# Two loads of the fourth row block of x are put behind a one-column memset on GpSimd

## The chip, the cores and the metric

The kernel runs on one core of a Trainium2 chip. The metric is the device time of one execution in microseconds (us). TensorE (PE, with its weight loads as PEld), VectorE (DVE), ScalarE (ACT), GpSimd (POOL) and SyncE (SP) run side by side. Transfers are issued from the queues of SP, ACT and POOL.

## What is computed

Two branches over the same input x (2048 rows of 512) are mixed by a gate, all in float32:

```python
def _A_ref(x, wqkv, w_phi, wo):          # linear attention, 32 heads of 16
    qkv = (lambda x, *d: x.transpose(*d))((x @ wqkv).reshape(B, S, 3, H, Dh), 2, 0, 3, 1, 4)
    q, k, v = qkv[0], qkv[1], qkv[2]
    pq = jnp.einsum("bhsd,hdf->bhsf", q, w_phi)
    pk = jnp.einsum("bhsd,hdf->bhsf", k, w_phi)
    phi_q = jnp.concatenate([_softmax(pq, axis=-1), _softmax(-pq, axis=-1)], axis=-1)
    phi_k = jnp.concatenate([_softmax(pk, axis=-1), _softmax(-pk, axis=-1)], axis=-1)
    kv = jnp.einsum("bhsf,bhsd->bhfd", phi_k, v)
    z  = jnp.einsum("bhsf->bhf", phi_k)
    num = jnp.einsum("bhqf,bhfd->bhqd", phi_q, kv)
    den = jnp.einsum("bhqf,bhf->bhq", phi_q, z)[..., None] + 1e-6
    o = num / den
    return (lambda x, *d: x.transpose(*d))(o, 0, 2, 1, 3).reshape(B, S, D) @ wo

def _B_ref(x, w1, b1, w2, b2):           # 512 -> 1792 -> 512, squared relu
    h = jnp.einsum("bsd,df->bsf", x, w1) + b1
    r = jnp.where(h > zero, h, zero)
    return jnp.einsum("bsf,fd->bsd", r * r, w2) + b2

g = _sigmoid((x * gate_w).sum(-1, keepdims=True))
return g * a + (1 - g) * b
```

## The kernel before

**Precision.** Each float32 operand is split into a high and a low part (`split`, lines 63 and 66: ACT copies the high part, DVE subtracts it from the source), and a product takes three matmuls (high by high, high by low, low by high). Such a triple stands at lines 76 to 78, or at 653 to 655 in the function `block`.

**Work in rounds.** x is cut into four blocks of 512 rows, b = 0 to 3, each as four tiles of 128x512 (k = 0 to 3). `work_list` walks twice over the four blocks, with seven of the fourteen chunks of the hidden layer each time. Each entry does an up product (`u`) and adds its down products into four sums (`d`). In the first walk the products for k and v run in between, for eight pairs of 128-row chunks (p = 0 to 7). The function `at(slot, f)` hangs each step on a half slot, and a scheduler makes one fixed order of instructions for each engine from it. An engine goes through its own list in order.

**A pair.** A pair p takes seven blocks of 128x512 products, i = 1, 2, 6, 5, 7, 3, 4, in banks pX and pY. Blocks 6, 7, 3 and 5 read sums and differences of x tiles instead of x. For these, `sums_load` (line 608) brings the pair's 128 rows of each x tile in two transfers of 256 KB, in runs of 512 bytes, and `sums_add` makes them with four additions, lines 615 to 618, on GpSimd for every pair but the first. `sums` then splits the result on ACT (`sh`) and DVE (`sl`).

**Weights that come back.** The weights of blocks 1, 6 and 3 don't stay on the chip. They lie in DRAM (`wkeep`, six tiles of 512 KB) and go round through three slots, named sloto twice (slots o0 and o1 here) and slotez. Once a tile has been used, `again` (line 641) issues from the ACT queue the load of the tile that is due three steps later into its slot. So within a pair block 1 reads o0 and o1, block 6 reads ez and then o0, block 3 reads o1 and then ez.

**The staging ring.** All transfers into tiles tagged `in` go through a ring of four buffers of 256 KB. A load waits until the splits or additions that read the buffer before are done. Around the change the ring is used in this order: the four tiles of x block 2 (loaded from the GpSimd queue, line 576), the two row tiles of pair 2, the four tiles of x block 3, and the two row tiles of pair 3. The loads of x block 3 are issued from the SP queue by the function `load`, line 86, called at line 582. Their first two tiles (k = 0, 1) take the buffers of the last two tiles of x block 2, and the other two (k = 2, 3) those of pair 2's rows. x block 3 is split at `x_split`, and first read by the products of pair 4.

Of the kernel before, what the change touches and what calls it, by code (L numbers as in the profile page):

```python
# [7 lines left out]
F32 = mybir.dt.float32  # L8
# [7 lines left out]
P = 128  # L16
S, D, H, DH, F = 2048, 512, 32, 16, 1792
NK = D // P
SB = 512
NB = S // SB  # L20
# [14 lines left out]
def tile_gated_mix(ctx: ExitStack, tc: tile.TileContext, xT, xn, wqT, wkT, wphi, wv, wo, w1, b1, w2, b2, gw, out):  # L35
    nc = tc.nc
    pool = lambda name, bufs, **kw: ctx.enter_context(tc.tile_pool(name=name, bufs=bufs, **kw))
    const = pool("const", 1)
    stage = pool("stage", 4)
# [44 lines left out]
    def load(src, eng=nc.sync):  # L84
        t = stage.tile([P, 512], F32, tag="in", name="in")
        st["in"] = eng.dma_start(t, src)
        return t
# [32 lines left out]
    st, up_w, down_w = {}, {}, {}  # L120
# [136 lines left out]
    def gate_load(n):  # L257
        eng, pin = ((nc.sync, "in" if n > 1 else "wv"), (nc.gpsimd, "summed"), (nc.sync, "ahead"), (nc.sync, "ahead"))[n // NC]
        st["xn", n] = row()
        with tc.issue_after(st[pin].ins):  # L260
            st["xrow"] = eng.dma_start(st["xn", n], xn[n])
# [308 lines left out]
    def x_load(b):  # L570
        if b == 2:
            st["xin", b] = []
            for k in range(NK):
                with tc.issue_after(st["summed"].ins):
                    t = stage.tile([P, 512], F32, tag="in", name="in")
                    st["summed"] = nc.gpsimd.dma_start(t, xT[b, :, k, :])
                    st["xin", b].append(t)
                if k > 1:
                    gate_load(NC + k)
                    st["summed"] = st["xrow"]  # L580
        else:
            st["xin", b] = [load(xT[b % NB, :, k, :]) for k in range(NK)]
        st["x", b] = []

    def x_split(b, k):
# [211 lines left out]
    for b in range(NB):  # L797
        for c in range(NC):
            s = b * SL + 2.5 * c - 1 if b > 1 else 17.5 + c / 2 if b else max(5.5, 3.5 + 2 * c)
            if b != 1 or c < 2:  # L800
                at(s, gate_load, b * NC + c)
            at(s + (4.5 if b == 1 else 3), gate_chunk, b * NC + c)
        if c == NC - 1:
            at(s + 4.5 if b == 1 else s + 3, gates, b)
        s, late = ((4, 2), (19.5, 1), (22, 2.5), (36, 2))[b]
        at(s, x_load, b + 1)
        for k in range(NK):
            at(s + late + k / 2, x_split, b + 1, k)
# [143 lines left out]
```

## Time and profile before

| | |
|---|---|
| time, median of 3 runs | 507.23 us (506.77 to 507.6) |
| the profiled execution | 507.18 us, of which the span from first to last instruction is 505.4 us |
| mean granted TensorE clock | 0.999 of full speed |
| busy: PE, PEld, DVE, ACT, POOL | 500.7, 406.1, 407.0, 256.6, 87.3 us |
| chain of work that ended last | PE 98%, DMA 1% |

All times below are counted from the start of the span. The span is 1.8 us shorter than the time of its execution. A busy TensorE is not a TensorE at its peak, since matmuls are pipelined: their recorded durations overlap, and the distance from one start to the next is what they cost.

### The profile page before, as it was taken

To read this page: it belongs to the slowest core of one execution; us is meant where nothing else is said; L and a number is where in the kernel's file an instruction comes from. 1 tells how busy PE (TensorE), PEld (TensorE's weight loads), DVE (VectorE), ACT (ScalarE), POOL (GpSimd) and SP (SyncE) were. 2 spreads that over 40 slices of the span, in tenths; PEclk is the share of its full clock that TensorE was granted. 3 is DMA by queue.
4 is the path that set the end of the run, shared out by engine and by line. 5 is a ranking of instruction groups with operands and counts; after the bars stand their busy time and mean duration, and the time that the engine had idled before them with its cause. 6 is when DMAs were issued, how large, how long until landed. Compare 5 with 4: busy or idle time off the path is not lost.

```text
span 505.4 us, 9354 instructions
## 1 busy us (share of the span) xinstructions
PE 500.7 (99%) x3520; PEld 406.1 (80%) x3520; DVE 407.0 (81%) x680; ACT 256.6 (51%) x458; POOL 87.3 (17%) x102
## 2 busy tenths in 40 slices
PE   9999999999999999999999999999999999999997
PEld 5878888788888888888888878788787878788776
DVE  5569957988695979796998989897979796897724
ACT  4887655565253474454674744454455353333540
POOL 1000151204410035000013040212222221112200
PEclk9999999999999999999999999999999999999999
DMA  8858587756854578771265311325112231041112
GB/s 261 291 196 273 198 305 225 237 190 234 285 184 165 183 223 294 265 228 65 83 211 209 98 49 48 99 64 150 49 31 90 71 86 43 8 131 57 38 27 83
DMA packets 45829, 76.13 MB, mean 151 GB/s; under 512 B 6868, under 2 KB 23000, under 8 KB 45784
## 3 DMA queue, kind: packets, MB, share of 16 engines
q1 hardware_dynamic: 36072, 41.78, 26.6%
q10 hardware_dynamic: 6768, 23.79, 13.7%
q0 software_dynamic: 2944, 9.96, 5.5%
q8 instruction: 28, 0.46, 0.4%
q14 instruction: 17, 0.14, 0.1%
HBM read 57.68 MB, written 11.54 MB: 137 GB/s over the span
## 4 chain that ended last, share of the span: by engine, by line
PE 98%; DMA 1%; DVE 0%; issue 0%
PE d L76 10%; PE d L77 10%; PE d L78 10%; PE u L76 10%; PE u L77 9%; PE u L78 9%; PE pX L653 3%; PE q L77 3%; PE att L77 3%; PE att L78 3%; PE att L76 3%; PE q L78 3%; PE q L76 3%; PE pX L655 3%; PE pX L654 3%; PE pY L655 2%
## 5 line engine op out<-in xcount | busy, mean ns | idle before, releaser
L421 ACT ACTIVATE r<-u,b1c 128x512 f32<-128x512 f32 x56 | 38.5, 687 | 122.9 <-PE u L78 121.2
L76 PE MATMUL d<-w2h,hh 128*128 128x512 f32 x222 | 86.9, 391 | 0.0
L77 PE MATMUL d<-w2l,hh 128*128 128x512 f32 x222 | 86.4, 389 | 0.0
L78 PE MATMUL d<-w2h,hl 128*128 128x512 f32 x222 | 86.4, 389 | 0.0
L76 PE MATMUL u<-xh,w1h 128*128 128x512 f32 x212 | 83.6, 394 | 0.0
L77 PE MATMUL u<-xl,w1h 128*128 128x512 f32 x212 | 82.6, 390 | 0.0
L78 PE MATMUL u<-xh,w1l 128*128 128x512 f32 x212 | 82.5, 389 | 0.0
L333 POOL TENSOR_TENSOR ez<-e,z 128x512 f32<-128x512 f32 x32 | 42.9, 1360 | 165.0 <-ACT e L309 165.0
L66 DVE TENSOR_TENSOR hl<-r,hh 128x512 fp32r<-128x512 f32 x56 | 37.8, 676 | 24.3 <-ACT hh L63 24.1
L76 PEld LDWEIGHTS d<-w2h,hh 128*128 128x128 f32 x222 | 41.7, 188 | 9.2 <-issue 0.6
L76 PEld LDWEIGHTS u<-xh,w1h 128*128 128x128 f32 x212 | 39.8, 188 | 11.1 <-issue 2.9
L78 PEld LDWEIGHTS d<-w2h,hl 128*128 128x128 f32 x222 | 41.7, 188 | 8.7
L77 PEld LDWEIGHTS d<-w2l,hh 128*128 128x128 f32 x222 | 41.7, 188 | 8.5
L78 PEld LDWEIGHTS u<-xh,w1l 128*128 128x128 f32 x212 | 39.8, 188 | 8.6 <-DVE w1l L66 0.2
L77 PEld LDWEIGHTS u<-xl,w1h 128*128 128x128 f32 x212 | 39.8, 188 | 7.9
L309 ACT ACTIVATE e<-e 128x1024 f32<-128x1024 f32 x27 | 28.6, 1059 | 26.5 <-DVE e L307 26.1
L291 DVE TENSOR_REDUCE sm<-e 128x64 f32<-128x1024 f32 x27 | 32.8, 1215 | 10.8 <-ACT e L309 10.8
L63 ACT ACTIVATE hh<-r 128x512 fp32r<-128x512 f32 x56 | 35.2, 628 | 1.1
L423 ACT ACTIVATE r<-r 128x512 f32<-128x512 f32 x56 | 34.9, 624 | 0.7
L692 ACT ACTIVATE tmp<-pX 128x512 f32<-128x512 f32 x24 | 14.4, 598 | 30.6 <-PE pX L655 27.0
L374 ACT ACTIVATE phiT<-tb 32x256 f32<-32x256 f32 x64 | 26.4, 412 | 5.8 <-DVE tb L359 4.9
L343 DVE TENSOR_REDUCE dz<-ez 128x64 f32<-128x1024 f32 x16 | 19.4, 1212 | 11.7 <-POOL ez L333 11.7
(182 smaller groups left out, 984.2 us busy)
## 6 DMA issues: line engine op xcount, KB each, us to landing
sloto<-wkeep ACTq DMA_DIRECT2D x30, 512.0 KB, 4.6
in<-in_xT SPq DMA_DIRECT2D x42, 256.0 KB, 4.4
slotez<-wkeep ACTq DMA_DIRECT2D x15, 512.0 KB, 5.0
phiT<-tb SPq DMA_DIRECT2D x192, 32.0 KB, 1.8
in<-in_w SPq DMA_DIRECT2D x23, 256.0 KB, 3.3
part<-row POOLq DMA_DIRECT2D x16, 256.0 KB, 5.5
row<-part SPq DMA_DIRECT2D x16, 256.0 KB, 3.0
out<-row SPq DMA_DIRECT2D x15, 256.0 KB, 2.2
```

Source lines behind the costliest of these rows:

```text
L63: i = nc.scalar.activation(hi, src, AF.Copy)
L66: st["lo"] = elo.tensor_tensor(lo, src, hi.bitcast(F32), ALU.subtract)
L76: nc.tensor.matmul(o, ah[:, sa], bh[:, sb], start=first, stop=False)
L77: nc.tensor.matmul(o, ah[:, sa], bl[:, sb], start=False, stop=False)
L78: return nc.tensor.matmul(o, al[:, sa], bh[:, sb], start=False, stop=last)
L291: nc.vector.tensor_reduce(sm, e3, AX.X, ALU.add)
L309: nc.scalar.activation(ef, ef, AF.Exp)
L333: nc.gpsimd.tensor_tensor(ez[:, hs, :], e3[:, hs, :], zbc[half], ALU.mult)
L374: nc.scalar.activation(dst, src, AF.Copy)
L421: st["relu"] = nc.scalar.activation(r, ps, AF.Relu, bias=b1c[:, fc:fc + 1])
L423: nc.scalar.activation(r, r, AF.Square)
L655: nc.tensor.matmul(ps, l, wh, start=False, stop=j == 1, skip_group_check=True)
```

## The change

When x block 3 is loaded, GpSimd writes a zero into the first column of each of the first two tiles (k = 0 and 1) before the transfer into that tile. The memset is ordered behind the instruction in `st["summed"]`, which at this point is the last addition of pair 2 (the third pair, p = 2), and the second memset behind the first. Each transfer overwrites the whole tile, so that it has to wait for the memset. The tiles k = 2 and 3, and the blocks 1 and 4, are loaded as before.

```diff
         else:
-            st["xin", b] = [load(xT[b % NB, :, k, :]) for k in range(NK)]
+            st["xin", b] = []
+            for k in range(NK):
+                t = stage.tile([P, 512], F32, tag="in", name="in")
+                if b == 3 and k < 2:
+                    with tc.issue_after(st["summed"].ins):
+                        st["summed"] = nc.gpsimd.memset(t[:, :1], 0.0)
+                st["in"] = nc.sync.dma_start(t, xT[b % NB, :, k, :])
+                st["xin", b].append(t)
```

The new lines move the rest of the file down by seven, and the loads of x now have line 588. GpSimd's list before, from pair 2's additions to the additions of the pair after it, which are for the row tiles called `in`:

```order
L615 TENSOR_TENSOR in<-in 128x2x128
L616 TENSOR_TENSOR in<-in 128x2x128
L617 TENSOR_TENSOR in<-in 128x2x128
L618 TENSOR_TENSOR in<-in 128x2x128
L615 TENSOR_TENSOR in<-in 128x2x128
L616 TENSOR_TENSOR in<-in 128x2x128
```

The same stretch of GpSimd's list in the change:

```order
L622 TENSOR_TENSOR in<-in 128x2x128
L623 TENSOR_TENSOR in<-in 128x2x128
L624 TENSOR_TENSOR in<-in 128x2x128
L625 TENSOR_TENSOR in<-in 128x2x128
L587 MEMSET in 128x1 x2
L622 TENSOR_TENSOR in<-in 128x2x128
```

The two memsets stand between the two pairs' additions, and nothing else moved on GpSimd. The SP queue's list in the difference between the two programs, from the pairs' row loads (128x4x128) over the loads of x block 3 (the four of 128x512) to the row loads of the next pairs:

```order
-L608 DMA in<-in_xT 128x4x128 x6
-L86 DMA in<-in_xT 128x512 x4
-L608 DMA in<-in_xT 128x4x128 x2
+L615 DMA in<-in_xT 128x4x128 x6
+L588 DMA in<-in_xT 128x512 x4
+L615 DMA in<-in_xT 128x4x128 x2
```

The order on SP is the same, with new line numbers. TensorE, VectorE and ScalarE keep their order too.

## Rows read from the trace of the kernel before

**Rows 1.** The page: span, engines (busy us, share, instructions), last chain by engine.
```profile
span 505.4 us, 9354 instructions
PE 500.7 (99%) x3520; PEld 406.1 (80%) x3520; DVE 407.0 (81%) x680; ACT 256.6 (51%) x458; POOL 87.3 (17%) x102
...
PE 98%; DMA 1%; DVE 0%; issue 0%
```

**Rows 2.** Waits of the weight loads: us in total, times, longest us.
```profile
PEld pX L653 <- DMA sloto<-wkeep: 0.6, 1, 0.6
```

**Rows 3.** The last chain in order of time, 90 to 98.7: start us, us.
```profile
90.99 6.89 DMA sloto<-wkeep
...
97.93 0.50 PE pX L653
```

**Rows 4.** Timeline of PE at block 1 of pair 2: start us, us.
```profile
96.93 0.39 PE L653 MATMUL pX<-sloto,xh 128*128 128x512 f32 x1
...
97.38 0.39 PE L655 MATMUL pX<-sloto,xl 128*128 128x512 f32 x1
...
98.26 0.39 PE L654 MATMUL pX<-sloto,xh 128*128 128x512 f32 x1
```

**Rows 5.** Line 86 (SP) and line 641 (ACT queue), a transfer each: issue, landing time.
```profile
L86 SPq DMA_DIRECT2D in<-in_xT x1: 353/353/353, 90.2 to 90.2; - x1
...
DMA to landing us min/median/max: 4.4/4.4/4.4
...
L86 SPq DMA_DIRECT2D in<-in_xT x1: 340/340/340, 91.7 to 91.7; - x1
...
DMA to landing us min/median/max: 6.4/6.4/6.4
...
L641 ACTq DMA_DIRECT2D slotez<-wkeep x1: 343/343/343, 91.7 to 91.7; - x1
...
DMA to landing us min/median/max: 7.3/7.3/7.3
```

**Rows 6.** Line 641 over the whole trace, all 45 loads.
```profile
DMA to landing us min/median/max: 3.1/4.7/8.2
```

**Rows 7.** Stretches of 2 us: busy us (instructions) by engine, PEclk, DMA share, GB/s.
```profile
94.00:96.00 2.00, 2.00 (x10) 1.67 (x9) 1.97 (x2) 0.37 (x1) 1.84 (x3) 1.00 0.99 385
96.00:98.00 2.00, 1.84 (x9) 1.20 (x7) 1.85 (x5) 1.49 (x3) 0.74 (x1) 1.00 0.48 190
98.00:100.00 2.00, 2.00 (x9) 1.65 (x10) 2.00 (x3) 1.97 (x5) 0.00 (x0) 1.00 0.38 140
```

**Rows 8.** Timeline of POOL: a first memset, pair 2's last addition, pair 3's first.
```profile
0.28 0.10 POOL L941 MEMSET const-float32-1.0<- 128x1 f32 x1
...
95.67 1.07 POOL L618 TENSOR_TENSOR in<-in 128x256 f32<-128x256 f32 x1
115.25 0.74 POOL L615 TENSOR_TENSOR in<-in 128x256 f32<-128x256 f32 x1 [18.51 <-DMA in<-in_xT]
```

**Rows 9.** Timeline of SP: x block 3's third load, then what follows its loads.
```profile
97.36 0.33 SPq L86 DMA_DIRECT2D in<-in_xT  x1
...
109.51 2.98 SPq L608 DMA_DIRECT2D in<-in_xT  x2
112.55 0.97 SPq L261 DMA_DIRECT2D row<-in_xn  x2
```

**Rows 10.** Timeline of ACT and its queue: start us, us, idle time before.
```profile
99.02 0.33 ACTq L641 DMA_DIRECT2D sloto<-wkeep  x1
...
99.63 0.33 ACTq L641 DMA_DIRECT2D sloto<-wkeep  x1
...
102.87 0.61 ACT L63 ACTIVATE xh<-in 128x512 fp32r<-128x512 f32 x1
...
105.75 0.60 ACT L692 ACTIVATE tmp<-pX 128x512 f32<-128x512 f32 x1 [2.26 <-PE pX L655]
```

**Rows 11.** Timeline of PEld at block 6 of pair 2.
```profile
104.64 0.19 PEld L653 LDWEIGHTS pX<-sloto,sh 128*128 128x128 f32 x1
```

## The prediction

> **What bounds the kernel now.** I read the page first, then the waits of TensorE, then the chain, and only then the queues around the place. The page says that TensorE is the kernel: it is busy for 500.7 of 505.4 us and holds 98% of the last chain, with 1% for a transfer [rows 1]. So only what lets TensorE start a matmul sooner or later counts. Among the waits of its weight loads there is one for a transfer, once, 0.6 us: the weight tile that comes back from wkeep into a slot o [rows 2]. The chain shows where: a load issued at 90.99 stands in it for 6.89 us, up to about 97.9, and the matmul at 97.93 follows [rows 3]. This is tile W[1,1], the second half of block 1 of pair 2, which goes into slot o1.
>
> What it costs is read from starts, since the recorded durations overlap. From 96.93 to 97.38 two steps take 0.45 us, or 0.225 each; from 97.38 to 98.26 two steps take 0.88 us [rows 4]. The loss is 0.88 - 0.45 = 0.43 us. (0.6 us is the idle time of the weight loads; they run ahead of the matmuls, so part of it costs nothing.) Without the wait the matmul would have started at 97.38 + 0.225 = 97.61. The transfer is only some 0.3 us late.
>
> What flies beside it: the first tile of x block 3, issued at 90.2 and landed 4.4 us later, the second, issued at 91.7 and landed 6.4 us later, and W[6,0] for slot ez, issued at 91.7 too and landed after 7.3 us [rows 5]. From 94 to 96 the transfer engines are busy for 0.99 of the time and move 385 GB/s; from 96 to 98 and 98 to 100 they are busy for 0.48 and 0.38 [rows 7]. So there is a full stretch, and behind it one with room. The two x tiles aren't wanted in either: ACT splits the first at 102.87 [rows 10].
>
> **The change part by part.**
>
> *The memsets.* Two instructions on GpSimd, each on 128x1 elements. A memset of this form took 0.10 us at the start of the span [rows 8]. Pair 2's last addition ends at 95.67 + 1.07 = 96.74, so both are done at about 96.95. Behind them on GpSimd stand pair 3's additions, which start at 115.25 after 18.51 us of waiting for their rows [rows 8]. That cover is 18 us thick: the memsets' own time costs nothing.
>
> *The two transfers.* They leave at about 97.0 and 97.5 instead of 90.2 and 91.7, two issues on SP taking 0.97 us [rows 9]. Behind them on the SP queue stands the third tile, issued at 97.36 before [rows 9]; it now leaves at about 98.0, 0.6 us later. After it come the fourth tile and then, only at 109.51, pair 3's rows [rows 9]. Nobody is held up: the first tile, even with the 6.4 us of its neighbour [rows 5], lands at 103.4, against the split at 102.87. In that worst case ACT is 0.5 us late, and it has 2.26 us of idle time before the next read of pX at 105.75 [rows 10]. With 4.4 us it lands at 101.4 and nobody notices. This edit costs 0; without the cover it would be the 0.5 us.
>
> *The transfer that was waited for.* W[1,1] now shares the full stretch with 512 KB less. At 385 GB/s these are 0.52 MB / 385 GB/s = 1.36 us if both tiles were ahead of its last bytes, and 0.68 us if only the first was, which left before it. So it lands at 97.9 - 1.36 = 96.5, or at 97.2. Both are before 97.61, and the wait goes: 0.43 us gained. The bounds come from all 45 loads of this line, 3.1 to 8.2 us [rows 6]: landed at 94.1, the gain is the same 0.43; with 8.2 us, at 99.2, the wait would be 1.3 us longer, but a transfer with less beside it has no reason to be slower than its 6.89, so I take 0 to 0.43 as the bounds of this term, and 0.43 as its value.
>
> *The transfers that now meet the two tiles.* At 99.02 and 99.63 ACT's queue issues W[6,1] for o0 and W[3,0] for o1 [rows 10]. W[6,1] is wanted first: its weight load starts at 104.64 [rows 11], and with the 0.43 us gained TensorE comes for it at 104.21. That leaves 104.21 - 99.02 = 5.2 us for it to land. (I don't let the issue move ahead: ACT comes to it through pair 2's additions and splits, not through TensorE.) Lines of this kind land after 3.1 us at the least, 4.7 in the median, 8.2 at most [rows 6]. Three x tiles, 0.79 MB, are now issued 1 to 2 us before it, of which at 385 GB/s some 0.4 MB should be through when it comes. I take the median, 4.7 us: landed at 103.7, 0.5 us to spare, cost 0. The ends are 0 and 104.21 to 99.02 + 8.2 = 107.2, which is 3.0 us of waiting.
>
> A page of the Trainium skill speaks against the change at just this place. DMA: Bandwidth & Descriptors, section Queues, rings and completion order, says that the increment of a transfer's semaphore is an ordered write, which lands only after all earlier writes of that DMA engine, also those of other queues. By it W[6,1] could not be reported before the three x tiles were written, whatever the share of its own queue; worked out from the rows' 385 GB/s, 0.79 + 0.52 MB from about 98 on are 3.4 us, or 101.4, and the sum would be the same. No run so far shows that order by itself.
>
> *The sum* is made against the profiled execution: 507.18 - 0.43 + 0 + 0 = 506.75 us. Its time is 0.05 us below the median of the three runs, 507.23, so beside that median I say **506.8 us**.
>
> **The rivals.**
>
> *The wait moves to W[6,1].* What speaks for it: the three tiles are bunched right in front of it, and its room shrinks to 5.2 us, 0.5 above the median. What speaks against it: the stretch from 96 to 100 has room [rows 7]. It costs from a landing of 5.2 us on; at 5.6 us the gain is used up, and at 6.6 us the kernel is 1.0 us slower. With the 7.3 us that W[6,0] took before in a full stretch [rows 5]: 99.02 + 7.3 - 104.21 = 2.1 us of waiting, 506.75 + 2.1 = 508.9 us. That is the rival on the other side. A mild form, 5.2 to 6 us, gives 506.8 to 507.6.
>
> *Nothing changes.* W[1,1] is late because of W[6,0], pair 2's rows and its own 512 KB, not because of the x tiles; then it lands at 97.6 to 97.9 and the time stays at 506.9 to 507.2. For it speaks that W[6,0], issued beside it, is as large as both tiles together. Against it: 0.3 us are enough to end the wait, and 0.68 us are taken off even in the poor case.
>
> *More than the wait is gained.* To be faster by over 0.2%, 1.0 us, more than twice the whole loss would have to go. No other wait of TensorE for a transfer stands in the trace [rows 2]; so the usual execution would have to wait longer there than the profiled one did. If it lost 1.1 us, the time would be 507.23 - 1.1 = 506.1 us.
>
> **How the numbers follow.** 0.2% of 507 us is 1.0 us, about what a measurement of this kernel can tell from no change; the three runs alone lie 0.8 us apart. The wait goes and nothing takes its place (506.8): 0.64. Nothing changes, or a mild wait eats the gain (506.9 to 507.6): 0.20. The wait on W[6,1] is long (508.9, over 508.2 in any case): 0.08. More is gained (506.1): 0.08. The first two lie within 0.2%; of the first I leave 0.03 to the scatter on the fast side and 0.01 on the slow side. That makes faster 0.11, same 0.80, slower 0.09. The range for 8 in 10 runs from 506.1, where the gain and the lower scatter of the runs (0.46 below the median) meet, to 507.6, the upper end of the runs shown and of the mild wait. It leaves out the long wait.
>
> **What would show it.** Right: TensorE starts steadily, 0.225 us apart, through block 1 of pair 2; no weight load waits for a slot o; the two x tiles are issued at about 97; W[1,1] lands in under 6.6 us; W[6,1] in under 5.2 us. Wrong: a weight load that waits at block 6 of pair 2, at about 104.2; ACT idle before the first split of x block 3; or W[1,1] still at 6.9 us. The prediction also falls if the memsets start well after 96.74, since each tenth that they lose pushes the x tiles closer to W[6,1].

## The result and the profile after

| | before | after |
|---|---|---|
| time, median of 7 runs each | 507.38 us (506.77 to 507.9) | 509.17 us (508.17 to 509.7) |
| ratio after to before | | 1.0034, 95% from 1.0023 to 1.0045 |
| the profiled execution | 507.18 us, span 505.4 us | 509.33 us, span 507.6 us |

The change makes the kernel 0.34% slower, some 1.8 us. The prediction of 506.8 us was wrong, and so was its sign. What came is the rival called "The wait moves to W[6,1]", which had a chance of 0.08 and a price of 508.9 us.

The page of the change, to be held against [rows 1]: the span, the engines with busy time and number of instructions, and the last chain by engine.

```profile
span 507.6 us, 9357 instructions
PE 501.5 (99%) x3520; PEld 406.5 (80%) x3520; DVE 406.6 (80%) x680; ACT 256.5 (51%) x458; POOL 87.2 (17%) x104
...
PE 95%; DMA 1%; DVE 1%; ACT 1%; POOL 1%; issue 0%; DVEq 0%
```

TensorE does the same 3520 matmuls, and no engine works longer by more than 0.8 us. But the chain that ended last now runs 5% of the span outside TensorE, through DVE, ACT, GpSimd and a transfer. The waits of the weight loads in the change say where it is left (total, times, longest); the line answers to [rows 2]:

```profile
PEld pX L660 <- DMA sloto<-wkeep: 2.0, 1, 2.0
```

It looks like the old wait, with 2.0 us for 0.6, but it is another tile. The timeline of PE in the change shows both places, block 1 first, and then block 6 of pair 2 (start, duration; in brackets the idle time before):

```profile
97.78 0.39 PE L662 MATMUL pX<-sloto,xl 128*128 128x512 f32 x1
98.01 0.39 PE L660 MATMUL pX<-sloto,xh 128*128 128x512 f32 x1
98.23 0.39 PE L661 MATMUL pX<-sloto,xh 128*128 128x512 f32 x1
...
104.36 0.39 PE L661 MATMUL pX<-slotez,sh 128*128 128x512 f32 x1
104.58 0.39 PE L662 MATMUL pX<-slotez,sl 128*128 128x512 f32 x1
106.55 0.50 PE L660 MATMUL pX<-sloto,sh 128*128 128x512 f32 x1 [1.58 <-DMA sloto<-wkeep]
106.88 0.40 PE L661 MATMUL pX<-sloto,sh 128*128 128x512 f32 x1
107.12 0.40 PE L662 MATMUL pX<-sloto,sl 128*128 128x512 f32 x1
```

At block 1, where one step took 0.55 us before (97.38 to 97.93, [rows 4] and [rows 3]), the starts now lie 0.23 and 0.22 us apart: that wait is gone. At block 6 one step takes 106.55 - 104.58 = 1.97 us instead of 0.23, so 1.74 us are lost, and the step behind it takes 0.33 us, another 0.1. These two make up most of the 2.16 us by which the last matmul of this execution starts later than that of the profile before (503.95 against 501.79).

The 0.43 us gained at block 1 don't show in the difference, because this execution came to block 1 late by 0.40 us: the up products already start 0.36 us later at about 10 us, and the same matmul of an earlier pair starts at 59.13 instead of 58.72, long before anything that was changed. Such shifts, up to 1 us among the profiles below, come and go from one execution to the next, in both kernels.

The chain of the change in order of time (start, duration) tells how the wait is fed:

```profile
94.18 0.73 POOL in L622
...
97.22 0.64 ACT sh L63
...
97.89 0.70 DVE sl L66
98.59 1.03 ACT tmp L309
99.62 0.58 ACT r L421
...
100.29 6.22 DMA sloto<-wkeep
...
106.55 0.50 PE pX L660
```

Pair 2's additions start at 94.18; through them, a split and two steps of ACT, W[6,1] is issued at 100.29, 6.1 us later, and takes 6.22 us. The weight load that needs the tile, in the timeline of PEld:

```profile
106.55 0.19 PEld L660 LDWEIGHTS pX<-sloto,sh 128*128 128x128 f32 x1 [2.00 <-DMA sloto<-wkeep]
```

TensorE came for it at 106.55 - 2.00 = 104.55, so there were 104.55 - 100.29 = 4.26 us of room.

What was in front of it stands in the timeline of POOL and in the transfers of lines 588 (x) and 648 (wkeep) in the change, to be held against [rows 8] and [rows 5]:

```profile
97.27 0.74 POOL L625 TENSOR_TENSOR in<-in 128x256 f32<-128x256 f32 x1
97.94 0.13 POOL L587 MEMSET in<- 128x1 f32 x2
```

```profile
L588 SPq DMA_DIRECT2D in<-in_xT x2: 340/340/341, 98.1 to 98.5; - x2
...
DMA to landing us min/median/max: 3.1/3.5/3.8
...
L588 SPq DMA_DIRECT2D in<-in_xT x1: 328/328/328, 99.4 to 99.4; - x1
...
DMA to landing us min/median/max: 4.7/4.7/4.7
...
L648 ACTq DMA_DIRECT2D sloto<-wkeep x1: 327/327/327, 91.4 to 91.4; - x1
...
DMA to landing us min/median/max: 4.0/4.0/4.0
```

Both memsets together take 0.13 us. The x tiles k = 0 and 1 leave at 98.1 and 98.5, the third tile at 99.4: 2.2, 1.7 and 0.9 us before W[6,1]. W[1,1], issued at 91.4, landed after 4.0 us instead of 6.89.

### The profile page after: what moved, and what is told of

Read it like the earlier page. It is cut to its first block, busy times and chain, and to the rows that moved or that the text cites. A ratio compares the mean times of both kernels' runs of the same rounds, so it can differ in the third digit from the quotient of the medians.

```text
span 507.6 us, 9357 instructions
## 1 busy us (share of the span) xinstructions
PE 501.5 (99%) x3520; PEld 406.5 (80%) x3520; DVE 406.6 (80%) x680; ACT 256.5 (51%) x458; POOL 87.2 (17%) x104
## 3 DMA queue, kind: packets, MB, share of 16 engines
q10 hardware_dynamic: 6768, 23.79, 13.7%
## 4 chain that ended last, share of the span: by engine, by line
PE 95%; DMA 1%; DVE 1%; ACT 1%; POOL 1%; issue 0%; DVEq 0%
PE d L76 10%; PE d L77 10%; PE d L78 10%; PE u L76 10%; PE u L78 9%; PE u L77 9%; PE pX L660 3%; PE q L76 3%; PE att L76 3%; PE att L78 3%; PE att L77 3%; PE q L77 3%; PE q L78 3%; PE pX L662 3%; PE pX L661 3%; PE pY L661 2%
```

## The experiments

The theory after the result: W[6,1] lands late because three x tiles (0.79 MB) are issued in the 2.2 us right in front of it. Its rivals: the memsets cost the time by themselves; W[6,1] is merely issued later than before; one part of the bunch, the two gated tiles or the third one behind them, does it alone; or the two queues, SP's and ACT's, get in each other's way whatever the distance. Kernels timed together share runs of the kernel before, and each ratio below is to those runs.

**The memsets without the gate** (`memset_aside`). They write into two spare columns, so that no transfer waits for them. The edits are against the change unless said otherwise.

```diff
-                        st["summed"] = nc.gpsimd.memset(t[:, :1], 0.0)
+                        st["summed"] = nc.gpsimd.memset(spare[:, k:k + 1], 0.0)
```

> The two memsets stand where the change has them, but write into two spare columns, so the two loads of x block 3 don't wait for them and leave at about 90.2 and 91.7 as before. Theory 1 (bunching: the two loads of x, moved to about 98, are in flight in front of W[6,1] and make it land late): time as before, 507.4 us, with the wait of about 0.6 us for W[1,1] back. Theory 2 (W[6,1] is issued late, because pair 2's rows land late and its additions and splits follow late; the x loads have no part in it): the additions are not touched by what the memsets write, so any time from 507.4 to 509.2 us is open. Theory 3 (the memsets themselves cost GpSimd or its port something): 509 us.

Measured: 507.15 us, ratio 0.9997 (0.9988 to 1.0006). The memsets are free, and the loss comes from the gate. The wait for W[1,1], which was expected back, doesn't show in the profile of this run.

**Only the second tile gated** (`k1_only`).

```diff
-                if b == 3 and k < 2:
+                if b == 3 and k == 1:
```

> Only the second tile (k = 1) of x block 3 waits for a memset; the first leaves at 90.2 as before. Theory 1: 256 KB less in front of W[6,1], which lands some 0.7 to 1.4 us sooner than in the change: a wait of 0.6 to 1.3 us instead of 2.0, and W[1,1] lands before it is wanted; 507.7 to 508.5 us. Theory 2: the time follows the issue of W[6,1] alone; as late as in the change, 509.2 us.

Measured: 508.15 us, ratio 1.0017 (1.0003 to 1.0031), half of the loss by the median, though the interval overlaps that of the change. In the chain of this run:

```profile
100.47 5.66 DMA sloto<-wkeep
```

W[6,1] has the tiles k = 1 and 2 at 2.2 and 1.3 us in front of it, lands after 5.7 us, and the wait is 1.1 us. By this run the loss grows with what stands in front.

**W[6,1] issued later, with nothing gated** (`pad`). In the kernel before, two additional additions of 128x128 into a spare tile stand ahead of pair 2's.

```diff
+            for j in range(2) if p == 2 else ():
+                add(spare, a1[:, j], d1[:, j], ALU.add)
             add(d1, a1, d1, ALU.add)
```

> The kernel before, with two extra additions of 128x128 on GpSimd (into a spare tile) ahead of pair 2's four, so that these, the splits behind them and the issue of W[6,1] come about 0.8 us later; the x loads stay at 90.2 and 91.7. Theory 1 (bunching): W[6,1] still lands within 4 to 5 us of its issue at about 99.9, before or at 104.9, so the time moves by 0.3 us at most, 507.4 to 507.7. Theory 2 (late issue is enough): a wait of 1 us and more at block 6 of pair 2, 508.5 to 509.2 us.

Measured: 508.06 us, ratio 1.0016 (1.0005 to 1.0027). In its chain and in its weight loads:

```profile
100.81 4.47 DMA sloto<-wkeep
```

```profile
105.32 0.19 PEld L656 LDWEIGHTS pX<-sloto,sh 128*128 128x128 f32 x1 [1.07 <-DMA sloto<-wkeep]
```

The tile landed after an ordinary 4.5 us, as the first theory had it, but had been wanted 105.32 - 1.07 - 100.81 = 3.44 us after its issue; the time lies between the ranges of the two theories. So the kernel before has nearly nothing to spare at this place: what the profile before showed as 5.2 us of room is usually less, and 0.8 us of time were lost by an issue that came later alone.

**The gated tiles behind W[6,1]** (`later_act`, repeated as `later_act_2`). The tiles are gated by one-column copies on ACT that stand behind the issue of W[6,1], and the loads of x block 3 are hung 1.5 slots later, so that the gate has an issue to refer to.

```diff
-                    with tc.issue_after(st["summed"].ins):
-                        st["summed"] = nc.gpsimd.memset(t[:, :1], 0.0)
+                    with tc.issue_after(st["back", 2, 0].ins), tc.high_priority(offset=AHEAD):
+                        nc.scalar.activation(t[:, :1], b1c[:, :1], AF.Copy)
...
-        s, late = ((4, 2), (19.5, 1), (22, 2.5), (36, 2))[b]
+        s, late = ((4, 2), (19.5, 1), (23.5, 1), (36, 2))[b]
```

> The two x tiles are gated by two one-column copies on ScalarE behind the issue of W[6,1] (instead of memsets on GpSimd in front of it), so they leave at about 101, after W[6,1] and before W[3,0]. Theory 1: W[6,1] has only the third x tile beside it, lands within 4.5 us, at 104.5 at the latest; both waits are gone and the time is 506.9 us, 0.4 to 0.6 below before. Theory 2: W[6,1] is issued at about 100.3 as in the change, and its wait stays: 508.5 to 509.2 us. A risk for both: the split of the first x tile on ScalarE comes at 103 to 104 and then has to wait for its load by 1 us.

> The kernel with the x tiles behind W[6,1] once more, with more rounds, to see whether it beats the kernel before. Theory 1: no wait at either place; 0.2 to 0.8 us below before, ratio 0.9985 to 0.9995. If the waits of before are mostly in other executions than the usual one: ratio 1.0.

Measured: 507.21 us, ratio 0.9993 (0.9981 to 1.0005), and in the repetition 507.51 us, 0.9989 (0.9976 to 1.0001). No weight load of either profile waits for a slot o. The load of W[6,1] in `later_act`:

```profile
L649 ACTq DMA_DIRECT2D sloto<-wkeep x1: 327/327/327, 100.2 to 100.2; - x1
...
DMA to landing us min/median/max: 3.6/3.6/3.6
```

Issued at the same moment as in the change (100.2 against 100.29), it lands after 3.6 us instead of 6.2. So a late issue isn't what the change adds; the kernel before issued W[6,1] at 100.36 and 100.54 in its two later profiles. That the tiles in front are the cause, this run alone doesn't show: W[3,0], issued 0.6 us behind W[6,1] in the change, comes 2.9 us behind it here. `two_front` below keeps it at 0.6. Whether this version beats the kernel before isn't settled: both intervals reach 1.

**Both kernels again** (`before_again` and `after_again`, one execution each).

> The kernel before once more, unchanged, for a second profile of it. If the profile that the prediction was read from is typical: pair 2's additions start 4.1 us after the kvps products of pair 0 end their wait, W[6,1] is issued at about 99 and W[1,1] makes TensorE wait for 0.6 us. If it was an early one: the additions start 4.6 to 5.0 us after, as in the profiles of the first four experiments, W[6,1] is issued at 100 or later, and the wait for W[1,1] is shorter or not there.

> The change once more, unchanged, for a second profile. Theory 1 (bunching): W[6,1] lands 6 us or more after its issue again, and TensorE waits for it by 1.5 to 2.5 us. If the first profile was a rare one: a wait under 1 us.

Measured: 507.99 and 508.01 us, so these two single executions were equal. Why, the rows say. First the weight load at block 6 and the start of pair 2's additions in the kernel before, then the weight load and the chain in the change:

```profile
105.54 0.19 PEld L653 LDWEIGHTS pX<-sloto,sh 128*128 128x128 f32 x1 [1.25 <-DMA sloto<-wkeep]
```

```profile
94.46 0.82 POOL L615 TENSOR_TENSOR in<-in 128x256 f32<-128x256 f32 x1 [11.85 <-DMA in<-in_xT]
```

```profile
105.53 0.19 PEld L660 LDWEIGHTS pX<-sloto,sh 128*128 128x128 f32 x1 [1.11 <-DMA sloto<-wkeep]
```

```profile
99.16 6.32 DMA sloto<-wkeep
```

The kernel before, too, can wait for W[6,1]: here its additions started at 94.46 (92.90 in the profile that the prediction was read from), the issue went to 100.36, and its weight load waited for 1.25 us with a landing of 5.1 us. The change had an early execution, with additions at 93.05 and the issue at 99.16, that is 5.3 us of room, and still waited for 1.11 us, since the landing took 6.3. It was the most room seen for the change, and not enough.

**W[6,1] on another queue** (`first_pool` and `early_pool_b`). In the first, GpSimd issues W[6,1] itself, ahead of the memsets, behind the additions; the loads of x hang at the slot of `later_act`. The second does the same to the kernel before, without a gate.

```diff
-                    with tc.issue_after(st["summed"].ins):
+                    with tc.issue_after(st["back", 2, 0].ins):
...
-        return tc.issue_after(nc.scalar.dma_start(t.bitcast(F32), wkeep[KEPT.index(k), jj]).ins)
+        eng = nc.gpsimd if (p, i, j) == (2, 1, 0) else nc.scalar
+        st["back", p, step] = eng.dma_start(t.bitcast(F32), wkeep[KEPT.index(k), jj])
+        return tc.issue_after(st["back", p, step].ins)
```

> W[6,1] is loaded from the GpSimd queue, behind pair 2's additions and ahead of the two memsets, so it leaves at about 98 and the x tiles half a microsecond after it. Theory 1: it leads the three x tiles, lands within 4 to 5.5 us, by 103.5, before it is wanted at about 104.5; no wait at block 6: 506.8 to 507.3 us. Theory 2 (the late issue on ScalarE is the larger part): also no wait, since the issue is 2 us sooner. If bytes alone decide, whatever the order in which they were issued: it lands with the x tiles after 6 us, at 104.2, just in time.

> The kernel before (x tiles at 90.2 and 91.7, no memset), with W[6,1] alone loaded from the GpSimd queue behind pair 2's additions. It is issued 2 us sooner than before, at about 98. If W[6,1] now and then makes TensorE wait in the kernel before too (its room is about 4.7 us in the later profiles, its landing 4.5 to 5): 0.1 to 0.4 us faster, 507.0 to 507.3. If only W[1,1] costs there: 507.4 us, no difference.

Measured: 507.43 us, ratio 0.9999 (0.9989 to 1.0008), and 507.39 us, 1.0 (0.999 to 1.001). The timeline of POOL in `first_pool`:

```profile
98.19 0.55 POOL L649 DMA_DIRECT2D sloto<-wkeep  x1 [0.20 <-issue]
98.74 0.15 POOL L587 MEMSET in<- 128x1 f32 x2
```

With W[6,1] in front of the tiles by half a microsecond it lands after 3.9 us, and the loss of the change is gone though both tiles are still gated and follow within 2 us. Two more things differ from the change: W[6,1] leaves 2 us sooner, and W[3,0] comes 2.7 us behind it. In `early_pool_b` it goes out at 98.9 and lands after 3.9 us too. An earlier issue in the kernel without the gate gains nothing in the median: its usual wait there is small.

**Which part of the bunch.** The change was timed again (`after_3`), the kernel before was timed against itself (`before_3`), and in `two_front` only the third tile (k = 2) is held back behind the issue of W[6,1], by a copy on ACT, so that the two gated tiles stand in front of it alone. The loads hang at the slot of `later_act` here too; W[3,0] still follows W[6,1] by 0.6 us.

```diff
+                if b == 3 and k == 2:
+                    with tc.issue_after(st["back", 2, 0].ins), tc.high_priority(offset=AHEAD):
+                        nc.scalar.activation(t[:, :1], b1c[:, :1], AF.Copy)
...
-        s, late = ((4, 2), (19.5, 1), (22, 2.5), (36, 2))[b]
+        s, late = ((4, 2), (19.5, 1), (23.5, 1), (36, 2))[b]
```

> The change once more, timed beside the kernel before with more rounds, and a third profile. Theory 1 (bunching) with what the second profiles showed (W[6,1] landed 6.2 and 6.3 us after its issue, at 100.3 and at 99.2): a landing of 6 us or more again, a wait of 1 to 2 us at block 6, and 508.5 to 509.2 us; the ratio to before stays above 1.002.

> The kernel before against itself: the ratio holds 1.0. A third profile of it. Theory 1 with a race: in each execution either pair 2's rows land early and W[1,1] late (a wait at block 1, as in the first profile) or the rows land late, W[6,1] is issued at 100 or later and may be waited for at block 6 (second profile), with a landing of W[6,1] of 5.1 us or less. A wait at both places, or a landing of 6 us with one x tile in front, speaks against it.

> The change, but with the third x tile (k = 2) gated by a one-column copy on ScalarE behind the issue of W[6,1]: two x tiles in front of W[6,1] instead of three. Theory 1 (each tile in front costs): W[6,1] lands 5.3 to 5.8 us after its issue instead of 6.2, the wait shrinks by 0.5 us or more, 508.2 to 508.7 us. If the two tiles of the change alone make the whole delay: 6.2 us and 509 us as in the change.

Measured: `after_3` 509.06 us, ratio 1.0022 (1.0008 to 1.0035); `before_3` 507.59 us, 0.9989 (0.9976 to 1.0001), so a batch can be off by some 0.1%; `two_front` 507.62 us, 0.9988 (0.9977 to 0.9998), the same as the kernel before against itself. The weight load in `after_3`, and then the load of W[6,1] in `two_front`:

```profile
106.13 0.19 PEld L660 LDWEIGHTS pX<-sloto,sh 128*128 128x128 f32 x1 [1.86 <-DMA sloto<-wkeep]
```

```profile
L651 ACTq DMA_DIRECT2D sloto<-wkeep x1: 326/326/326, 100.3 to 100.3; - x1
...
DMA to landing us min/median/max: 4.1/4.1/4.1
```

With all three tiles in front, 6.2 us and a wait of 1.86 us; with the two gated ones at 98.0 and 98.5 and without the third, 4.1 us and no wait. (TensorE came late in this execution of `two_front`, with its weight load of slot o0 at 105.60, and it was late already in the first pairs; but with 4.1 us W[6,1] was there at 104.3, before the 104.55 at which the change came for it.) The two gated tiles by themselves cost nothing. That is neither branch of what was expected: taking one tile away saved 2.1 us of landing, and not 0.4 to 0.9, so a price for each tile is not how it works.

**The third tile alone** (`k2_late`), and **the three spread out** (`early_gate`). It was open whether the third tile, the nearest to W[6,1], does it alone. In `k2_late` the first two leave as before, and the third waits for a memset of the whole tile behind the additions. In `early_gate` the two memsets stand behind the second of pair 2's four additions (its edit is shown against the kernel before).

```diff
-                if b == 3 and k < 2:
+                if b == 3 and k == 2:
...
-                        st["summed"] = nc.gpsimd.memset(t[:, :1], 0.0)
+                        st["summed"] = nc.gpsimd.memset(t, 0.0)
```

```diff
+                t = st["first"][k] if b == 3 and k < 2 else stage.tile([P, 512], F32, tag="in", name="in")
...
-            add(a1, a0, a1, ALU.subtract)
+            st["second"] = add(a1, a0, a1, ALU.subtract)
+            if p == 2:
...
+                for t in st["first"]:
+                    with tc.issue_after(st["second"].ins):
+                        st["second"] = nc.gpsimd.memset(t[:, :1], 0.0)
             add(a0, d1, a0, ALU.subtract)
```

> The kernel before, with the first two x tiles free as before (90.2 and 91.7) and only the third (k = 2) held back by a full-tile memset on GpSimd, so that it leaves about 0.7 us later than before, some 1 us ahead of W[6,1] instead of 1.7. Theory A (the third tile decides: the change pushes it down the SP queue until it runs into W[6,1]): W[6,1] lands 5.5 to 6.2 us after its issue, a wait of 0.8 to 1.8 us at block 6, 508.2 to 509 us. Theory B (the bytes of all three tiles): one tile in front as before, landing 4.1 to 5.1 us, 507.3 to 507.7 us.

> The change with its two memsets behind pair 2's second addition instead of the fourth. The two tiles leave about 2 us sooner, at about 96, so the third isn't pushed and leaves at about 98.8, 1.6 us ahead of W[6,1]. Theory A: W[6,1] lands within 5.1 us as in before; W[1,1] has landed by 96.5 and isn't waited for: 507.0 to 507.4 us. Theory B: the same 0.79 MB are in front of W[6,1], two of the three tiles 2 us farther ahead; a landing of 5 to 5.6 us and 507.6 to 508.3 us.

Measured: `k2_late` 507.34 us, ratio 0.9998 (0.9987 to 1.001); `early_gate` 507.51 us, 0.9997 (0.9987 to 1.0006). The weight load at block 6 in `k2_late`, then that in `early_gate` and its chain:

```profile
104.55 0.19 PEld L660 LDWEIGHTS pX<-sloto,sh 128*128 128x128 f32 x1 [0.21 <-DMA sloto<-wkeep]
```

```profile
105.93 0.19 PEld L662 LDWEIGHTS pX<-sloto,sh 128*128 128x128 f32 x1 [0.81 <-DMA sloto<-wkeep]
```

```profile
101.13 4.76 DMA sloto<-wkeep
```

In `k2_late` the third tile left at 99.5 and W[6,1] at 100.49; it landed some 4.0 us later, at the end of the wait of 0.21 us. So the third tile alone doesn't do it either, and that theory falls. In `early_gate` the same three tiles left at 97.3, 97.8 and 99.5, ahead of an issue at 101.13, and W[6,1] took 4.8 us. The loss in the median is gone, though the same three tiles are in front, the first two some 1.6 us farther ahead. The landing is as theory A had it, the median between the two theories' ranges; the profiled execution, with its late issue, was the slowest of its twelve (508.38 us).

## Why the prediction was wrong, by its steps

The landings of W[6,1], from the rows above and the same rows of the runs named, by what x block 3 has issued in the 4 us in front of it. The last column is what the ACT queue, which carries W[6,1], moved in the first 2 us after the issue:

| in front of W[6,1], us before it | landed after, us | moved in 2 us, MB |
|---|---|---|
| third tile, 1.6 (`later_act`, `later_act_2`; W[3,0] 2.9 us behind) | 3.6, 3.9 | 0.18, 0.18 |
| third tile, 1.6 (`pad`, `before_again`) | 4.5, 5.1 | 0.17, 0.19 |
| third tile, 1.0 (`k2_late`) | 4.0 | 0.05 |
| first and second, 2.2 and 1.7 (`two_front`) | 4.1 | 0.11 |
| second and third, 2.2 and 1.3 (`k1_only`) | 5.7 | 0.05 |
| all three, 3.9, 3.3, 1.6 (`early_gate`) | 4.8 | 0.08 |
| all three, 2.2, 1.7, 0.9 (the change; `after_3`, `after_again`) | 6.2; 6.2, 6.3 | 0; 0, 0 |

*The memsets* were right: 0.13 us for both, and nothing lost (`memset_aside`).

*The two transfers* were right in their distances: the prediction had the three tiles 2.0, 1.5 and 1.0 us ahead of W[6,1]; 2.2, 1.7 and 0.9 were measured. The first tile landed at 101.2, where 101.4 was forecast, and its split on ACT didn't wait for it.

*The transfer that was waited for* was right as a mechanism: W[1,1] lands after 4.0 us (4.6 in `after_3`, 5.9 in `after_again`; 5.1 to 6.9 in the three profiles of the kernel before) and its wait is gone. But its size, 0.43 us, was that of one execution. Of the seven profiled executions in which the first two tiles left at 90 to 93 us as before (`memset_aside`, `pad`, `early_pool_b` and `k2_late` among them), only the first waited for W[1,1]. In `before_again` the wait of the kernel before was on W[6,1], and `before_3` shows none at either place. What isn't lost as a rule can't be won as a rule.

*The transfers that now meet the two tiles*: this is the step that failed. "I take the median, 4.7 us: landed at 103.7, 0.5 us to spare, cost 0." The landing was 6.2 to 6.3 us in three executions of the change. The median of all 45 loads of the line [rows 6] takes in loads with and without company; the loads of this size that fly with company were in [rows 3] and [rows 5], and they took 6.89 and 7.3. The prediction said that some 0.4 MB should be through when W[6,1] comes, at the 385 GB/s of a full stretch. In the change it was 0.28 MB. The windows of 2 us of the change and then of the kernel before in `before_3` (the last two columns are the busy share of the transfer engines and GB/s):

```profile
96.00:98.00 2.00, 2.00 (x10) 1.66 (x9) 0.71 (x2) 0.63 (x1) 1.84 (x5) 1.00 0.03 10
98.00:100.00 2.00, 2.00 (x10) 1.68 (x9) 2.00 (x5) 1.96 (x3) 0.08 (x3) 1.00 0.25 89
100.00:102.00 2.00, 2.00 (x10) 1.65 (x10) 2.00 (x3) 1.83 (x4) 0.00 (x0) 1.00 0.73 238
102.00:104.00 2.00, 2.00 (x11) 1.65 (x10) 2.00 (x4) 0.81 (x1) 0.00 (x0) 1.00 0.52 130
104.00:106.00 2.00, 0.97 (x5) 0.47 (x3) 2.00 (x5) 0.78 (x2) 0.00 (x0) 1.00 1.01 412
```

```profile
96.00:98.00 2.00, 2.00 (x11) 1.65 (x10) 0.04 (x1) 0.52 (x1) 1.84 (x3) 1.00 0.73 287
...
100.00:102.00 2.00, 2.00 (x10) 1.66 (x9) 2.00 (x4) 1.97 (x4) 0.00 (x0) 1.00 0.64 157
102.00:104.00 2.00, 2.00 (x11) 1.65 (x10) 2.00 (x4) 0.67 (x2) 0.00 (x0) 1.00 0.91 332
```

Without the gate the engines work from 96 to 98 (0.73), and when W[6,1] comes they are nearly free for it: 332 GB/s from 102 to 104. With the gate they stand still from 96 to 98 (0.03), and by 100 only 89 GB/s x 2 us = 0.18 MB have been moved of the three tiles' 0.79. The stretch with room was left empty, and its bytes were put in front of the one transfer that TensorE wants next. The clock (1.00) plays no part.

Where W[6,1] loses its time can be read from the queues. All 45 loads of wkeep, 23.6 MB, go out from ACT, and q10 is the only queue with about that sum on the page (23.79 MB). q1 carries the x tiles: what it moves in the change from 98 to 104.3 adds up to the three tiles' 0.79 MB. In the 2 us after the issue of W[6,1], first in the change (100.29 to 102.29: all packets, then q1), then in `before_3` (100.54 to 102.54):

```profile
DMA packets 232, 0.42 MB, mean 210 GB/s; under 512 B 30, under 2 KB 30, under 8 KB 231
q1 hardware_dynamic: 231, 0.41, 73.1%
```

```profile
q10 hardware_dynamic: 42, 0.17, 48.7%
q1 hardware_dynamic: 88, 0.15, 21.7%
```

In the change q10 moves nothing in this time. Its first packet starts at 103.0, 2.7 us after the issue (2.3 and 2.4 in `after_3` and `after_again`), where in `before_again`, `before_3`, `pad` and `memset_aside` it starts after 1.0 us. From its first packet on it lands within 3.5 to 3.9 us, where `pad` and `before_again` took 3.5 and 4.2. So most of the loss lies ahead of its first packet, which starts 1.3 to 1.7 us later, while the x tiles go out at 0.41 MB in 2 us, some 205 GB/s and not 385. (In the stretch of 385 GB/s, 94 to 96 in the profile before, q10 had moved 0.58 MB and q1 0.19.)

The other half of this step, the room, was read too wide. 5.2 us come from a profile whose additions started at 92.90 and whose W[6,1] went out at 99.02. In the other executions here, those of the experiments included, the additions start between 93.05 and 95.0, and where ACT issues W[6,1] it goes out at 99.2 to 101.1, some 6 us behind (7.2 in `pad`). Of the change's three profiles the room was 4.26, 4.35 and 5.3. That is not the change's doing, as the kernel before shows the same, but it decides how much of 6.2 us is felt: the waits were 2.0, 1.86 and 1.11 us.

*The rival* had the place and the mechanism, and 2.1 us of waiting by a landing of 7.3 against 5.2 of room; it was a landing of 6.2 against 4.3, so about the same price; both were about a microsecond lower, and that the price came out so close is luck. It was given too small a chance because its landing was held against the median row and not against the rows with company.

*The page that spoke against the change*, of the Trainium skill: DMA: Bandwidth & Descriptors, section Queues, rings and completion order, by which a transfer's semaphore is written only after all earlier writes of the DMA engine, across queues. The trace doesn't contradict it: the third tile landed at 99.4 + 4.7 = 104.1, W[6,1] at 106.5. By the rule alone it could have come 2.4 us sooner, and what is late here is the data of W[6,1] itself, which starts to move at 103.0, and not only the report of it; in `two_front` and `k2_late` tiles stand ahead of it on the other queue without harm. So no run here shows that this order is the cause.

What stays open: why W[6,1] doesn't start beside the x tiles, although the transfer engines are busy for only 0.52 of the time from 102 to 104 and run at 412 GB/s behind that; and why in `k2_late`, where its first packet starts 1.7 us after the issue, it still lands after 4.0 us. That three tiles in 2.2 us cost 2 us of landing, where the first two without the third, or the third without them, cost nothing, is measured; what makes it so isn't shown. Whether holding the tiles back behind W[6,1] (`later_act`) is worth 0.1% isn't settled.

## What to carry to other kernels

A transfer that is held back doesn't disappear: look for the next transfer that the bottleneck engine wants, and price its landing by rows of transfers that fly with the same company, not by the median of its line. Slack read from one profile is one draw: before spending 0.5 us of it, ask what sets the issue and the demand, and how far each moves between executions. If a load must be put off, put it behind the urgent one in issue order (`later_act` and `first_pool` lost nothing), not behind a compute step that happens to end just ahead of it.

## What the runs showed of the hardware

Landing times didn't add up: 512 KB from wkeep landed after 4.1 us with two 256 KB loads of another queue 2.2 and 1.7 us ahead, after 4.0 with one load 1.0 us ahead, and after 6.2 to 6.3 with all three. About half the distance made the difference between 4.8 and 6.2 us. With all three within 2.2 us in front, the first packet of its queue started 2.3 to 2.7 us after the issue instead of 1.0. And the start of pair 2's additions, which wait for the landing of their rows or for DVE, moved between 92.9 and 95.0 us from execution to execution, with no change in the program ahead of it.
